# Handing memory and PSUM from the forward to the backward recurrence tile by tile, with the last row sum inside the first backward block and a buffer of its own for the last softmax

## The chip, the cores and the metric

The kernel runs on one core of one Trainium2 chip. The metric is the device time of one execution in microseconds. The core has a matrix engine (TensorE, "PE" in the profile, its weight loads "PEld"), a vector engine (VectorE, "DVE"), an activation engine (ScalarE, "ACT"), a general engine (GpSimd, "POOL"), and SyncE ("SP"), which here issues DMA transfers. Each engine works through its own queue of instructions in the order in which they were written; engines wait for each other by semaphores. Matrix products land in PSUM, which has eight banks of 128 partitions by 2 KB; everything else on the core lies in SBUF.

## The reference

What is computed is a forward pass and the gradients of all of its inputs for a given grad_out. The forward pass, cut to what matters (S = 2048 tokens, Dm = 512, 32 heads of 128, M = 8 memory tokens, segments of 32 tokens, F = 1792):

```python
xn  = layernorm(x)
mem = mem0                                  # 8 rows
for s in range(64):                         # segments of 32 tokens
    h = concat(mem, xn[32*s : 32*s+32])     # 40 rows
    q, k, v = h @ Wq, h @ Wk, h @ Wv        # 32 heads of 128
    p = softmax(where(mask, q @ k.T * scale, -1e9))
    o = (p @ v) @ Wo
    mem = o[:8]                             # goes to the next segment
    outs.append(o[8:])
r   = relu(xn @ w1 + b1)
out = x + concat(outs) + (r * r) @ w2 + b2
# then: vjp of all this for grad_out, for x, mem0, Wq, Wk, Wv, Wo, w1, b1, w2, b2
```

The memory rows make the forward pass a chain through 64 segments, and the backward pass a chain through the same segments in reverse order.

## The kernel before

The kernel has four stages, one after the other: the squared-ReLU layer forward and backward; the forward recurrence; the backward recurrence; and the weight gradients as large matrix products (L2042). The 64 segments are worked in 16 blocks of four (SPB = 4, TC = 16). "L" in names such as `l_attn`, `qLN`, `PLL`, `RFL` means work on a block's memory rows and other edges of its segments, done for a whole block at once; "A" means work on the 32 token rows of a segment.

**Order.** Both recurrences are planned with `_Beat` (L487). Each operation has keys for what it reads and writes, and a due time from a table: `_FWD` or `_BWD`, each with three tables, for the middle blocks, the first block and the last one. A value is a due time in nanoseconds times 4, plus in its last two bits the engine that takes the operation, where more than one can. An operation of block b is due at its table value plus b times the beat (58,393 or 64,984 ns). Operations whose predecessors are done are written out in order of due time, and that order is each engine's queue, SyncE's and GpSimd's transfers among them. `plan.at = (block, slot group)` says which block an operation belongs to. There are two plans, one for each recurrence, and the second is written out behind the first.

**Forward, around its end.** `chain` (L1422) does a segment's attention, `l_proj` and `l_attn` (L1376) the memory rows of a block, `blk_out` the block's normalized rows. PA holds in its two halves the transposed token rows of two blocks, the half being the block number modulo 2, and the transposed grad_out of two blocks in the backward pass (names hA and gT). The token rows of the attention's result go to DRAM (S_RO) in parts; `out_sum(b)` (L1331) loads them back into `sumR` in two halves, adds them on GpSimd (L1338, L1340) to the rows of the other branch (`sumB`, loaded from S_B) and stores the sum as output. For the last block its four transfers are put on GpSimd's queue. `softmax` (L1290) takes the row maximum, subtracts it (L1296), takes the exponential, sums, and divides; in the form for memory rows ("L") the intermediate `st` is not a buffer of its own but `sumR`:

```python
sm_t[sfx] = [... mx, sm ...] + [tl("stA", ...)[:] if sfx == "A" else
                sumR[:].rearrange("p y d -> p (y d)").rearrange("p (i k) -> p i k", i=NI)]
```

so that `out_sum` and the memory rows' softmax share the key `stL`. At the end of the forward plan `turn` (L750) transposes Wv in place, in groups of eight 128x128 matmuls (L688) through a PSUM bank and back by one VectorE or ScalarE copy (L692, L694), and `turn_o` does the same to Wo, with two copies a group. Wo lies in the tile WB, Wq, Wk and Wv in WA.

**Backward.** It begins with 32 such groups for Wk and Wq, of which nine stand ahead of the first matmul of the recurrence and the others among it. `l_pre` (L1671) loads a block's grad_out transposed (`dmaT`, L1666) and does the memory rows' part, `load` (L1789) fetches a segment's q, k, v and softmax, `chain` (L1803) follows a segment backward, `l_post` (L1709) forms a block's gradients for memory rows and stores to S_GN and others; one store to S_RL belongs to each block. The block-diagonal operands BDP, BDL, BDS, BDK are set to zero once (L1619) and then filled by small copies (L928, L934). The weight turns of both plans take PSUM banks from rings.

**Memory.** Each recurrence opens its own SBUF pool (`fw` L1238, `bw` L1587) and its own PSUM pool (`pc`, `pc2` L1589). The second pair takes the space of the first, so the first use of any of its tiles waits for the release of what lay there.

Of the kernel before, what the change touches and what calls it, by code (L numbers as in the profile page):

```python
# [10 lines left out]
ALU = mybir.AluOpType  # L11
# [67 lines left out]
    ),  # L79
    (  # L80
# [82 lines left out]
    ),  # L163
)
_FWD_BEAT = 58393
_BWD = (
    (
# [1937 lines left out]
```

## Time and profile before

| | |
|---|---|
| median of 3 runs | 2857.02 us (2855.41 to 2859.66) |
| the profiled execution's own time | 2858.51 us |
| its span, first to last instruction | 2856.7 us |
| mean granted TensorE clock | 0.994 |
| TensorE busy | 2688.5 us, 94% of the span |
| VectorE, ScalarE, GpSimd busy | 1611.3, 1189.5, 939.8 us |

One execution was recorded by the hardware profiler. Its page gives the busy time of each engine, the span in slices, the chain of work that ended last, and the costliest groups of instructions by source line. Beside the page the trace can be asked for the timeline of an engine in a stretch of time, for what each engine waited for (and which instruction or transfer released it), and for a table of stretches with each engine's busy time, the granted clock as a share of full speed, the DMA share and GB/s. Times count from the start of the span. In a timeline a line is: start, duration, engine, source line, operation, output <- inputs, shape, count, and in brackets the idle time before it with its releaser. "SPq" is a transfer's issue on SyncE's queue.

### The profile page before, as it was taken

How to read it: one execution, taken by the hardware profiler on the slowest of the kernel's cores; microseconds unless marked ns; L12 is line 12 of the kernel's file. 1: busy time of each engine (PE TensorE's matmuls, PEld its weight loads, DVE VectorE, ACT ScalarE, POOL GpSimd, SP SyncE). 2: the span in 40 equal slices, each digit the busy share in tenths (PEclk: the TensorE clock that was granted, in tenths of full speed). 3: DMA queues.
4: the chain of work that ended last, by engine and by line, in shares of the span. 5: the costliest groups of instructions: out<-in, count | busy, mean ns of one | idle time of the engine just before them, and what ended most of it. 6: DMA issues, size and time to landing. Idle time of an engine off the chain costs nothing. (4 is left out here: it accounts for less than half of the span.)

```text
span 2856.7 us, 113933 instructions
## 1 busy us (share of the span) xinstructions
PE 2688.5 (94%) x47469; PEld 1556.2 (54%) x47640; DVE 1611.3 (56%) x4769; ACT 1189.5 (42%) x2781; POOL 939.8 (33%) x2630
## 2 busy tenths in 40 slices
PE   8998999999999999789999999999999899999999
PEld 6664565555656555565555555555555444444444
DVE  5645667666666667566566666666666602232322
ACT  4333455455545555455555555555555400000000
POOL 1102223222322223344455554545454301111111
PEclk9999999999999999999999999999999999999999
DMA  6657768777777765368889898888888799788861
GB/s 195 213 170 200 199 196 215 207 199 200 207 203 210 200 187 165 118 149 216 221 230 240 226 236 235 232 224 232 221 233 214 207 358 298 229 255 266 253 185 43
DMA packets 557595, 606.26 MB, mean 212 GB/s; under 512 B 229925, under 2 KB 358454, under 8 KB 555030
## 3 DMA queue, kind: packets, MB, share of 16 engines
q1 hardware_dynamic: 541654, 544.09, 69.0%
q0 software_dynamic: 15424, 54.87, 5.7%
q8 instruction: 374, 6.13, 1.0%
q14 instruction: 143, 1.17, 0.2%
HBM read 290.14 MB, written 272.12 MB: 197 GB/s over the span
## 5 line engine op out<-in xcount | busy, mean ns | idle before, releaser
L802 PE MATMUL ps<-WA,PA 128*32 128x512 bf16 x6144 | 366.8, 379 | 5.5 <-DVE PA L1490 3.7
L2042 PE MATMUL ps<-WA,WB 128*128 128x512 bf16 x1505 | 330.7, 379 | 2.2 <-DVE gwo L692 0.6
L802 PEld LDWEIGHTS <-PA 128*32 128x32 bf16 x8192 | 207.3, 96 | 202.5 <-issue 12.2
L2042 PEld LDWEIGHTS <-WB 128*128 128x128 bf16 x1896 | 185.5, 98 | 224.4 <-issue 0.9
L692 DVE CAST gwo<-ps 128x512 bf16<-128x512 f32 x64 | 40.0, 683 | 398.9 <-PE ps L2042 267.2
L1660 PE MATMUL ps<-WA,dT 128*32 128x512 bf16 x4096 | 248.2, 382 | 9.7 <-DVE dT L785 8.0
L694 ACT CAST dN<-ps 128x512 bf16<-128x512 f32 x356 | 206.0, 586 | 108.9 <-PE ps L912 77.3
L694 ACT CAST gwo<-ps 128x512 bf16<-128x512 f32 x64 | 33.1, 599 | 517.2 <-PE ps L2042 357.9
L928 POOL COPY BDA<-PB 32x128 bf16<-32x128 bf16 x287 | 82.6, 288 | 413.8 <-DVE PLp L1458 266.8
L2053 POOL DMA_DIRECT2D out_dram<-gwo x96 | 71.3, 751 | 294.2 <-ACT gwo L694 263.4
L1660 PEld LDWEIGHTS <-dT 128*32 128x32 bf16 x4096 | 94.2, 97 | 125.8 <-DVE dT L785 46.8
L785 DVE STREAM_TRANSPOSE dT<-dN 128x256 f32<-128x256 f32 x256 | 109.4, 434 | 68.3 <-ACT dN L694 65.8
L934 POOL COPY BDL<-dSL 32x64 bf16<-32x64 bf16 x256 | 61.5, 240 | 255.9 <-PE ps L912 234.3
L1316 PE MATMUL ps<-WB,OT 128*32 128x256 bf16 x4096 | 134.1, 278 | 5.0 <-DVE OT L785 4.7
L802 PE MATMUL ps<-WB,PA 128*32 128x512 bf16 x2048 | 125.5, 381 | 6.6 <-issue 5.8
L1660 PE MATMUL ps<-WA,gOT 128*32 128x512 bf16 x2048 | 128.0, 380 | 1.2 <-DVE gOT L785 0.9
L934 POOL COPY BDP<-bP 32x256 bf16<-32x256 bf16 x256 | 106.7, 417 | 67.7 <-ACT BDP L928 16.3
L1542 PE MATMUL ps<-sx,anT 128*128 128x512 bf16 x352 | 116.1, 380 | 10.5 <-issue 4.3
L1316 PEld LDWEIGHTS <-OT 128*32 128x32 bf16 x4096 | 101.6, 98 | 42.2 <-DVE OT L785 32.5
L694 ACT CAST gON<-ps 128x512 bf16<-128x512 f32 x123 | 72.0, 585 | 107.7 <-PE ps L802 96.6
L928 POOL COPY BDS<-maskA 32x128 bf16<-32x128 bf16 x249 | 72.0, 289 | 128.4 <-DVE maskA L1846 122.6
L802 PE MATMUL ps<-WA,PB 128*32 128x512 bf16 x1536 | 113.4, 380 | 0.0
(320 smaller groups left out, 5753.8 us busy)
## 6 DMA issues: line engine op xcount, KB each, us to landing
S_GN<-dN SPq DMA_DIRECT2D x192, 256.0 KB
WA<-S_GN SPq DMA_DIRECT2D x160, 256.0 KB
S_K<-kN SPq DMA_DIRECT2D x64, 256.0 KB
S_Q<-qN SPq DMA_DIRECT2D x64, 256.0 KB
S_V<-vN SPq DMA_DIRECT2D x64, 256.0 KB
S_ON<-oN SPq DMA_DIRECT2D x64, 256.0 KB
bqN<-S_Q SPq DMA_DIRECT2D x64, 256.0 KB
xs<-S_Q SPq DMA_DIRECT2D x64, 256.0 KB
```

The costliest lines, as they stand in the source:

```text
L692: nc.vector.tensor_copy(out, in_)
L694: nc.scalar.copy(out, in_)
L785: self.plan.add({"DVE": 0.36}, lambda e, x=x: nc.vector.transpose(dst[:, x, :, :].rearrange("p i c r -> p (i c r)").bitcast(F32).rearrange ...
L802: nc.tensor.matmul(bk()[32 * j:32 * (j + 1), :], lhsT=win(dc), rhs=Wt(dc, c0), start=(dc == 0), stop=(dc == DC - 1), tile_position=(0, 32 ...
L928: self.plan.add({"ACT": 0.31, "DVE": 0.2, "POOL": 0.31}, lambda e, j=j: {"ACT": nc.scalar.copy, "DVE": nc.vector.tensor_copy, "POOL": nc.g ...
L934: self.plan.add(cost or {"ACT": 0.4, "DVE": 0.27, "POOL": 0.42}, lambda e, j=j: {"ACT": nc.scalar.copy, "DVE": nc.vector.tensor_copy, "POO ...
L1316: nc.tensor.matmul(bk()[32 * t:32 * (t + 1), :], lhsT=tq(OTt, i, j), rhs=Wo[:, JQ * i + j, h * HB:(h + 1) * HB], start=(i == 0 and j < 2), ...
L1542: A(pe(0.217, "f", 0.11), lambda e, c=c, z=z, x=x: nc.tensor.matmul(bks[x]()[:], lhsT=anT[x][:, c, :], rhs=sx[z][:], start=(c == 0), stop= ...
L1660: nc.tensor.matmul(bk()[32 * j:32 * (j + 1), :], lhsT=tq(XT, i, j), rhs=wtf(t, i, j), start=(first and i == 0), stop=(last and i == NI - 1 ...
L2042: nc.tensor.matmul(bks[n]()[:], lhsT=HNc[:, rc, dc * P:(dc + 1) * P], rhs=half_of(gns[y], hf), start=(y == 0), stop=(y == NRC - 1))
L2053: q.dma_start(outWs[t][dc * P:(dc + 1) * P, hf, :, j], wt[:].rearrange("p (i e) -> p i e", i=4))
```

## The change

- **Tiles that live through both recurrences.** One SBUF pool `px` and one PSUM pool with all eight banks (`ps_all`) are opened before the forward recurrence and closed after the backward one. The tiles of px have neutral names: XK (2), XA, XN (8), XH (3), BDA, BDB, PLp. Forward names (KT, qLT, vLN, lN, PLL, sumR, sumB, hN, anT, sx, wt) and backward names (gN, qN, kN, VR, VT, Pt, btA, PLL, VTL, kLN, LT, dN, dT, gOT, xs, ys, R_A, BDL, BDK) are views of them; `dSp` is PLp, BDP and BDS are BDA and BDB. The pools `fw` and `bw` keep what is left.
- **Last sum.** `out_sum(15)` is taken out of the last forward block and put at the start of the backward plan, in the first block's table under a slot group of its own (`plan.at = (0, -2)`). Its transfers are on SyncE's queue.
- **Last softmax.** In block 15 the memory rows' softmax takes `stX`, the first part of anT (tile XA), in place of the buffer that `out_sum` uses.
- **Parity.** The backward halves are chosen by (b + 1) % 2 in place of b % 2, so that block 15's transposed grad_out goes to the half of PA that block 14 had.
- **Zeroing.** Of the four memsets of BDP, BDL, BDS, BDK two are left (BDL, BDK), written in the forward plan's last block; those of dSp go. The mask's scratch tile mk becomes a view of WA.
- **Tables.** The tables are given anew in steps a hundred times finer (beats 5,839,300 and 6,498,400). The forward middle table is the old one times 100, for a fifth of its values up to rounding, and orders the operations as before. The tables of the first and last forward block and all backward tables differ in order; in a middle backward block 27 operations change engine.

The diff, cut to its core:

```diff
-    with tc.tile_pool(name="fw", bufs=1) as fw, \
-            tc.tile_pool(name="pc", bufs=1, space=bass.MemoryType.PSUM) as pc:
+    px_cm = tc.tile_pool(name="px", bufs=1)
+    px = px_cm.__enter__()
+    pc_cm = tc.tile_pool(name="pc", bufs=1, space=bass.MemoryType.PSUM)
+    pc = pc_cm.__enter__()
+    ps_all = pc.tile([P, 8, 512], F32, name="ps")
+    XK = [px.tile([P, SPB * NI * JQ * KA], BF16, name="XK%d" % x) for x in range(2)]
+    XA = px.tile([P, 7 * HW], BF16, name="XA")
+    XN = [px.tile([P, HW], BF16, name="XN%d" % x) for x in range(8)]
+    XH = [px.tile([P, HW // 2], BF16, name="XH%d" % x) for x in range(3)]
+    BDA, BDB = (px.tile([P, NI, JQ, RA], BF16, name=n) for n in ("BDA", "BDB"))
...
+    def out_sum(sg, b, sumR, rk, sumB, bk):
+        A = sg.plan.add
+        sumR = sumR[:].bitcast(F32).rearrange("p (y d) -> p y d", y=2)
+        sg.dma(lambda: sumB, lambda: S_B[b * P:(b + 1) * P, :], [], bk)
+        for h in range(2):
+            sg.dma(lambda h=h: sumR, lambda h=h: S_RO[b, h].rearrange("y p d -> p y d"),
+                   [("RO", b, v) for v in range(SPB)] + [("RO", b, "L")], [rk])
+            A({"POOL": 0.9}, lambda e: nc.gpsimd.tensor_tensor(
+                out=sumR[:, 0, :], in0=sumR[:, 0, :], in1=sumR[:, 1, :], op=ALU.add), [], [rk])
+            A({"POOL": 0.9}, lambda e, h=h: nc.gpsimd.tensor_tensor(
+                out=sumB[:, h * HB:(h + 1) * HB], in0=sumR[:, 0, :], in1=sumB[:, h * HB:(h + 1) * HB], op=ALU.add),
+              [rk], bk)
+        sg.dma(lambda: out0flat[b * P:(b + 1) * P, :], lambda: sumB, bk, [])
+
+    with tc.tile_pool(name="fw", bufs=1) as fw:
...
+        stX = XA[:, 0:HW].bitcast(F32).rearrange("p (i k) -> p i k", i=NI)
...
+            if own:
+                st, k = stX, lambda n: ("anT", 0, 0) if n == "st" else n + sfx
...
-            softmax("L", bk, 2 * RL, PLL, "PLL", 1, (0.72, 0.64, 0.71))
+            softmax("L", bk, 2 * RL, PLL, "PLL", 1, (0.72, 0.64, 0.71), b == TC - 1)
...
-            out_sum(b, tail)
+            if not tail:
+                out_sum(sg, b, XN[7], "stL", XH[1][:], ["sumB"])
...
+        BDL, BDK = (tr4(XK[0], x * HW) for x in range(2))
+        for x, t_ in enumerate((BDL, BDK)):
+            A({"POOL": 0.95}, lambda e, t_=t_: nc.gpsimd.memset(t_, 0.0), ...)
...
-    pc2_cm = tc.tile_pool(name="pc2", bufs=1, space=bass.MemoryType.PSUM)
-    pc = pc2_cm.__enter__()
...
-        for t_ in (BDP, BDL, BDS, BDK):
-            nc.gpsimd.memset(t_[:], 0.0)
+        BDP, BDS = BDA, BDB
...
         def l_pre(b):
             plan.at = (TC - 1 - b, 0)
-            p = b % 2
+            p = (b + 1) % 2
...
+        plan.at = (0, -2)
+        out_sum(sg, TC - 1, xs[0], ("xs", 0), XN[6][:, 0:D], [("ys", 0), ("ys", 1)])
         sg.rings = {"t": [("c", 4), ("f", 1)], "f": [("f", 0)]}
         for t, nm in ((1, "Wk"), (0, "Wq")):
             sg.turn("t", nm, Wqkv[t], nm, (t, "WT"))
         l_pre(TC - 1)
```

More of the change, by code (lines that the diff above doesn't have):

```diff
@@ L967 @@
     NEG = -1e9
[L968 to L969 removed]
+    mk = WA[:, 0:RA]
+    nc.gpsimd.memset(mk, 0.0)
     for j in range(JQ):
@@ new lines, with nat, tr4 @@
+    PLp = []
+    for v in range(SPB):
+        t_ = (px.tile([P, NI, RL], BF16, name="PLp%d" % v)[:] if v + 1 < SPB else
+              pb_rest[:, HW // 2:HW // 2 + NI * RL].rearrange("p (i k) -> p i k", i=NI))
+        if v + 1 < SPB:
+            nc.vector.memset(t_, 0.0)
+        PLp.append(t_)
+    def nat(t, at=0):
+        return t[:, at:at + HW].rearrange("p (i e) -> p i e", i=NI)
+    def tr4(t, at=0):
+        return t[:, at:at + HW].rearrange("p (i j r) -> p i j r", i=NI, j=JQ)
+    def out_sum(sg, b, sumR, rk, sumB, bk):
[11 more added lines that the diff above has]
+        sg.dma(lambda: out0flat[b * P:(b + 1) * P, :], lambda: sumB, bk, [])
@@ L1254 @@
         xL = inL
-        KT = [tl("KT%d" % x, [P, SPB, NI * JQ, KA]) for x in range(2)]
-        qLT = [tl("qLT%d" % x, TR) for x in range(2)]
-        vLN = [tl("vLN%d" % x, NAT) for x in range(2)]
-        lN0, lN1 = (tl(n, NAT) for n in ("lN0", "lN1"))
+        KT = [XK[x][:].rearrange("p (v a k) -> p v a k", v=SPB, k=KA) for x in range(2)]
+        qLT = [tr4(XN[x]) for x in range(2)]
+        vLN = [nat(XN[2 + x]) for x in range(2)]
+        lN0, lN1 = nat(XN[4]), nat(XN[5])
         VM = lN1
@@ L1264 @@
         PTA, PTL = (pb_rest[:, x * HW // 4:(x + 1) * HW // 4].rearrange("p (i k) -> p i k", i=NI) for x in range(2))
-        PLL, PTLL = tl("PLL", [P, NI, 2 * RL]), tl("PTLL", [P, NI, 2, RL])
-        BDA, BDB = (tl(n, [P, NI, JQ, RA]) for n in ("BDA", "BDB"))
+        PLL = XN[6][:, 0:HW // 2].rearrange("p (i k) -> p i k", i=NI)
+        PTLL = XN[6][:, HW // 2:HW].rearrange("p (i c k) -> p i c k", i=NI, c=2)
         for t_ in (BDA, BDB):
             nc.gpsimd.memset(t_[:], 0.0)
-        RFA, RFL = tl("RFA", [P, HB], F32), tl("RFL", [P, HB], F32)
+        RFA, RFL = tl("RFA", [P, HB], F32), XH[0][:].bitcast(F32)
         selF = tl("selF", [P, 2 * M], F32)
@@ L1277 @@
             )
-        sumR, sumB = tl("sumR", [P, 2, HB], F32), tl("sumB", [P, D])
-        hN = tl("hN", [P, D])
+        hN = XH[2]
         sm_t = {}
@@ L1282, with softmax @@
             sm_t[sfx] = [tl(n + sfx, [P, NI], F32) for n in ("mx", "sm")] + [tl("stA", [P, NI, nk], F32)[:] if sfx == "A" else
-                            sumR[:].rearrange("p y d -> p (y d)").rearrange("p (i k) -> p i k", i=NI)]
+                            XN[7][:].bitcast(F32).rearrange("p (i k) -> p i k", i=NI)]
+        stX = XA[:, 0:HW].bitcast(F32).rearrange("p (i k) -> p i k", i=NI)
         plan = _Beat(tc, _FWD_BEAT, TC, _FWD)
-        sg = Stage(plan, {"c": (0, 4), "f": (4, 2), "m": (6, 2)}, pc.tile([P, 8, 512], F32, name="ps"), 0.9)
+        sg = Stage(plan, {"c": (0, 4), "f": (4, 2), "m": (6, 2)}, ps_all, 0.9)
         A = plan.add
         V = nc.vector
-        def softmax(sfx, bk, nk, Pout, pkey, prio, cA):
+        def softmax(sfx, bk, nk, Pout, pkey, prio, cA, own=False):
             mx, sm, st = sm_t[sfx]
@@ L1329, in wo_part @@
                   [bk.key], [(okey, half)], prio, 0.07)
-        def out_sum(b, tail):
-            q = "POOL" if tail else "SP"
-            c = T_DMA + tail
-            sg.dma(lambda: sumB[:], lambda: S_B[b * P:(b + 1) * P, :], [], ["sumB"], cost=c, eng=q)
-            for h in range(2):
-                sg.dma(lambda h=h: sumR[:], lambda h=h: S_RO[b, h].rearrange("y p d -> p y d"),
-                       [("RO", b, v) for v in range(SPB)] + [("RO", b, "L")], ["stL"], cost=c, eng=q)
-                A({"POOL": 0.9}, lambda e: nc.gpsimd.tensor_tensor(
-                    out=sumR[:, 0, :], in0=sumR[:, 0, :], in1=sumR[:, 1, :], op=ALU.add), [], ["stL"])
-                A({"POOL": 0.9}, lambda e, h=h: nc.gpsimd.tensor_tensor(
-                    out=sumB[:, h * HB:(h + 1) * HB], in0=sumR[:, 0, :], in1=sumB[:, h * HB:(h + 1) * HB], op=ALU.add),
-                  ["stL"], ["sumB"])
-            sg.dma(lambda: out0flat[b * P:(b + 1) * P, :], lambda: sumB[:], ["sumB"], [], cost=c, eng=q)
         def l_proj(b):
@@ L1417, in l_attn @@
             sg.dma(lambda: S_RO[b].rearrange("h y (v r) d -> (h y) v r d", r=RA)[:, :, 0:M],
-                   lambda: RFL[:], ["RFL"] + [("RO", b, v) for v in range(SPB)], [("RO", b, "L")],
+                   lambda: RFL, ["RFL"] + [("RO", b, v) for v in range(SPB)], [("RO", b, "L")],
                    cost=T_DMA + tail, eng="POOL" if tail else "SP")
-            out_sum(b, tail)
+            if not tail:
+                out_sum(sg, b, XN[7], "stL", XH[1][:], ["sumB"])
         def chain(s):
@@ L1520, in blk_out @@
                        cost=T_DMA + tail, eng="POOL" if tail else "SP")
-        anT = [tl("anT%d" % x, [P, TC, P]) for x in range(2)]
-        sx = [tl("sx%d" % x, [P, D]) for x in range(5)]
-        wt = tl("wt", [P, D])
-        wtT = wt[:].rearrange("p (c f) -> p c f", c=DC)
+        anT = [XA[:, 2 * HW * x:2 * HW * (x + 1)].rearrange("p (c f) -> p c f", c=TC) for x in range(2)]
+        sx = [XA[:, 4 * HW + x * D:4 * HW + (x + 1) * D] for x in range(5)]
+        wt = XA[:, 4 * HW + 5 * D:7 * HW]
+        wtT = wt.rearrange("p (c f) -> p c f", c=DC)
         def dw_unit(which, u):
@@ L1582 @@
         plan.at = (TC - 1, -1)
+        BDL, BDK = (tr4(XK[0], x * HW) for x in range(2))
+        for x, t_ in enumerate((BDL, BDK)):
+            A({"POOL": 0.95}, lambda e, t_=t_: nc.gpsimd.memset(t_, 0.0), [("KTL", 0, 0)] if x else [],
+              [("KTL", 0, h) for h in range(2)] + [("KTA", 0, v, h) for v in range(SPB) for h in range(2)] if x == 0 else [("bd", 1)])
         sg.turn("m", "Wv", Wqkv[2], ("WA", 2), "WvT")
@@ L1596 @@
         TR = [P, NI, JQ, RA]
-        dSp = []
-        for v in range(SPB):
-            t_ = (tl("dSp%d" % v, [P, NI, RL])[:] if v + 1 < SPB else
-                  pb_rest[:, HW // 2:HW // 2 + NI * RL].rearrange("p (i k) -> p i k", i=NI))
-            nc.vector.memset(t_, 0.0)
-            dSp.append(t_)
+        dSp = PLp
         gT = inA
         gL = inL
-        qLN, kLN, gLN = ([tl(n + "%d" % x, NAT) for x in range(2)] for n in ("bqLN", "bkLN", "gLN"))
-        VTL = [tl("VTL%d" % x, TR) for x in range(2)]
@@ L1607 @@
-        PLL, dSL = ([tl(n + "%d" % x, [P, NI, 2 * RL]) for x in range(2)] for n in ("bPLL", "dSL"))
-        LT0, LT1, LT2 = (tl("LT%d" % x, TR) for x in range(3))
-        VTM, VR = LT1, tl("VR", TR)
+        at = lambda x, n: XA[:, x:x + n]
+        halves = lambda t: t.rearrange("p (i k) -> p i k", i=NI)
+        gN, qN, kN = (nat(XA, x * HW) for x in range(3))
+        VR = tr4(XA, 3 * HW)
+        VT = at(4 * HW, NI * JQ * KA).rearrange("p (i j k) -> p i j k", i=NI, j=JQ)
+        x0 = 4 * HW + NI * JQ * KA
@@ new lines @@
+        Pt = [halves(at(x0 + x * NI * KA, NI * KA)) for x in range(2)]
+        btA = halves(at(x0 + 2 * NI * KA, 2 * NI * KA).bitcast(F32))
+        x0 += 4 * NI * KA
+        PLL = [halves(at(x0, HW // 2)), halves(XH[1][:])]
+        assert x0 + HW // 2 == 7 * HW
+        dSL = [tl("dSL", [P, NI, 2 * RL])[:], halves(XH[0][:])]
+        qLN, gLN = ([tl(n + "%d" % x, NAT)[:] for x in range(2)] for n in ("bqLN", "gLN"))
+        VTL, kLN = [tr4(XK[0], 2 * HW), tl("VTL", TR)[:]], [nat(XK[0], 4 * HW), tl("bkLN", NAT)[:]]
@@ L1610 @@
+        LT0, LT1, LT2 = tr4(XK[1]), tr4(XK[0], 3 * HW), tr4(XN[3])
+        VTM = LT1
         dLN = tl("dLN", NAT)
         KM = dLN
-        dSTLL = tl("dSTLL", [P, NI, 2, RL])
+        dSTLL = XH[2][:].rearrange("p (i c k) -> p i c k", i=NI, c=2)
         brL = tl("brL", [P, NI], F32)
-        xs = [tl("xs%d" % x, [P, HW]) for x in range(JQ)]
+        xs = [XN[x] for x in (1, 4, 5, 7)]
         btL = xs[3][:].bitcast(F32).rearrange("p (i k) -> p i k", i=NI)
-        ys = [tl("ys%d" % x, [P, NI * RL]) for x in range(JQ)]
@@ L1617 @@
-        BDP, BDL, BDS, BDK = (tl(n, [P, NI, JQ, RA]) for n in ("BDP", "BDL", "BDS", "BDK"))
-        for t_ in (BDP, BDL, BDS, BDK):
-            nc.gpsimd.memset(t_[:], 0.0)
-        qN, kN, gN = (tl(n, NAT) for n in ("bqN", "bkN", "gON"))
-        VT, gOT = tl("bVT", [P, NI, JQ, KA]), tl("gOT", TR)
-        Pt = [tl("bP%d" % x, [P, NI, KA]) for x in range(2)]
-        btA, brA = tl("btA", [P, NI, KA], F32), tl("brA", [P, NI], F32)
+        ys = [XN[6][:, x * NI * RL:(x + 1) * NI * RL] for x in range(JQ)]
```

50 lines of the change are left out of this document (22 added, 28 removed), and 601 rows, old and new, of tables (_BWD, _FWD).

## The prediction

> **What bounds the kernel now.** I read the page first for the engine that sets the time, then the table of stretches for the place where that engine stops, then the timelines of TensorE, VectorE and SyncE at that place.
>
> ```profile
> span 2856.7 us, 113933 instructions
> PE 2688.5 (94%) x47469; PEld 1556.2 (54%) x47640; DVE 1611.3 (56%) x4769; ACT 1189.5 (42%) x2781; POOL 939.8 (33%) x2630
> ```
>
> TensorE is busy for 94% of the span, so a change can win only where TensorE stands still. The table of stretches (busy time of TensorE, its weight loads, VectorE, ScalarE, GpSimd, then the granted clock) shows where that is:
>
> ```profile
> 1130.00:1190.00 60.00, 51.88 (x1260) 33.85 (x1249) 39.48 (x118) 28.52 (x66) 19.67 (x55) 1.00 0.38 122
> 1340.00:2250.00 910.00, 856.06 (x19484) 497.43 (x19484) 579.43 (x1811) 495.99 (x1150) 458.89 (x1420) 1.00 0.87 229
> 1193.60:1201.90 8.30, 0.06 (x1) 0.00 (x0) 1.30 (x3) 0.58 (x2) 2.14 (x4) 0.67 0.53 159
> 1211.50:1228.40 16.90, 9.56 (x132) 8.71 (x129) 11.27 (x19) 7.99 (x15) 5.36 (x8) 0.86 0.21 59
> 1228.40:1236.20 7.80, 7.01 (x72) 6.43 (x71) 3.72 (x7) 2.02 (x2) 4.66 (x5) 0.65 0.90 134
> 1236.20:1265.40 29.20, 27.91 (x606) 20.59 (x606) 22.72 (x54) 18.11 (x28) 11.84 (x38) 1.00 0.74 182
> ```
>
> The steady backward recurrence (second row) runs at 94%. The seam between the recurrences does not: TensorE works 0.06 us of 8.30 just before 1201.9, then 9.56 us of 16.90 in the turn of Wo. The change edits that seam. Its TensorE timeline (start, duration, line, operation, in brackets the idle time ahead and what ended it):
>
> ```profile
> 1193.05 0.61 PE L688 MATMUL ps<-ident,WA 128*128 128x128 bf16 x8 [0.31 <-ACT WA L694]
> 1201.94 1.01 PE L688 MATMUL ps<-ident,WA 128*128 128x128 bf16 x8 [8.28 <-DVE WA L692]
> 1207.67 0.24 PE L868 MATMUL ps<-vLN,PTLL 32*32 32x128 bf16 x4
> 1211.53 2.41 PE L688 MATMUL ps<-ident,WB 128*128 128x128 bf16 x40
> 1217.58 4.09 PE L688 MATMUL ps<-ident,WB 128*128 128x128 bf16 x48 [2.40 <-ACT WB L694]
> 1228.43 2.80 PE L688 MATMUL ps<-ident,WA 128*128 128x128 bf16 x24 [1.59 <-DVE WB L692]
> 1236.23 0.62 PE L802 MATMUL ps<-WB,PB 128*32 128x512 bf16 x8
> ```
>
> So the path here is: eight idle microseconds, rest of the forward pass (1201.94 to 1211.53), Wo's turn (1211.53 to 1228.43), nine Wk groups (1228.43 to 1236.23), first backward chain. What holds TensorE at 1193.7 is a queue behind a queue, read from the other engines' timelines and the table of waits (total, times, longest):
>
> ```profile
> 1191.33 0.69 DVE L1295 TENSOR_REDUCE mxL<-ps 128x8 f32<-128x512 f32 x1
> 1200.60 0.69 DVE L1296 TENSOR_TENSOR sumR<-ps,mxL 128x512 f32<-128x512 f32 x1 [8.58 <-POOL sumB L1340]
> 1199.10 0.72 POOL L1338 TENSOR_TENSOR sumR<-sumR 128x256 f32<-128x256 f32 x1 [3.87 <-DMA sumR<-S_RO]
> 1199.90 0.67 POOL L1340 TENSOR_TENSOR sumB<-sumR,sumB 128x256 bf16<-128x256 f32 x1
> 1196.16 0.41 SPq L748 DMA_DIRECT2D sumR<-S_RO  x1
> 1192.09 1.50 SPq L1667 DMA_TRANSPOSE PA<-in_grad_out_dram  x1
> SPq L1667 <- PE ps L688: 16.2, 1, 16.2
> SPq L748 <- DMA out_dram<-sumB: 18.4, 1, 18.4
> 1228.64 0.32 SPq L748 DMA_DIRECT2D bqN<-S_Q  x1
> 1228.40 0.94 POOL L1619 MEMSET BDP<- 128x1024 bf16 x1 [1.62 <-DVE WB L692]
> ```
>
> SyncE stands 16.2 us at the transposing load of block 15's gradient, because that load's half of PA is still read by block 15 itself. Behind it in SyncE's queue lies the second load of out_sum(14) (1196.16). GpSimd adds it into sumR until 1200.5, and sumR is also the buffer in which the last softmax subtracts its maximum (L1296). VectorE waits in order, the Wv evictions behind it wait, TensorE finds no free bank. The second SyncE row is the other barrier: the first backward load (1228.64) stood 18.4 us for the pools that the forward recurrence gives up, until out_sum(15) had stored its rows.
>
> **The change, part by part.** Own softmax buffer and turned block parity. The last softmax writes anT's first part, unused by then, and block 15's gradient goes to the half of PA that block 14 has left. Both locks go together: L1296 can follow L1295 at 1192.0 instead of 1200.6, 8.6 us earlier; the parity removes what would be late next, the VM loads and out_sum(14)'s load behind SyncE's block. After 1201.94 nothing was waiting for anything but this (forward matmuls and the softmax chain), so the stretch from 1201.94 to 1211.53 moves as a whole: lower end 8.3 us (the idle time), upper end 8.6 plus what the slow clock cost. For that, two rows of the same matmul shape and the clock:
>
> ```profile
> 1188.46 0.62 PE L1316 MATMUL ps<-WB,OT 128*32 128x256 bf16 x16
> 1202.88 1.04 PE L1316 MATMUL ps<-WB,OT 128*32 128x256 bf16 x16
> 1200.00:1210.00 10.00, 7.14 (x156) 5.21 (x159) 6.59 (x12) 4.58 (x7) 3.03 (x6) 0.67 0.55 187
> ```
>
> At 0.62/1.04 the 7.14 us of TensorE work in that row would be 4.3: up to 2.9 us more. I take 9.0 in all, since the softmax chain on VectorE and ScalarE, not TensorE's rate, orders most of those 10 us. Ends: 8.3 and 11.5.
> [...]
>
> Shared tiles and banks, so no barrier between pools. Before, the nine Wk groups belong to the second plan and follow Wo's turn. In the written order of the changed program 6 of the 9 lie between Wo's groups and only 3 behind them, then the first chain. Wo's turn itself had room: 16.90 us with 9.56 of TensorE, 11.27 of VectorE, 7.99 of ScalarE. The 6 groups bring 6 evictions and two thirds of 7.01 us of matmul at clock 0.65, about 3.0 us at full clock. VectorE and ScalarE did 3.72 + 2.02 = 5.74 us in the row of the nine groups, so six cost at most 3.8 on the two. Free time there is 5.6 us of VectorE, 8.9 of ScalarE, 7.3 of TensorE, so they fit: cost 0, or 1.9 if both evicting engines are the bound in turn. Behind the turn, 3 groups take a third of 7.80, 2.6 us: 5.2 gained. Net 5.2 at the best, 3.3 at the worst; I take 4.5, nearer the best because the free time is twice the need.
> The loads that began at 1228.64 and the memsets from 1228.40 are hidden then: two memsets are left of four GpSimd ones (0.94 each) and lie in idle GpSimd time. The four VectorE memsets of dSp go too. That earlier loads help the first block (1236.20 to 1265.40, TensorE 27.91 of 29.20) I count as 0: at most 1.3 us of idle time could go. If a load comes late in the new order instead, it costs up to one landing, 2.9 us (SyncE's 1196.16 to GpSimd's 1199.10).
>
> out_sum(15). Its two store-gated loads, the load of S_B and the store move from GpSimd's queue (at the tail) to SyncE's, its four adds into the first backward block. GpSimd: 2 x (0.72 + 0.67) = 2.8 us in a stretch where it is busy 11.84 of 29.20; hidden, upper end 2.8. SyncE: four issues of about 0.4, and the first S_RO load stands behind RFL's store on GpSimd, with kN, P and qN loads queued behind it. Before, that store stood here:
>
> ```profile
> 1212.68 0.55 POOL L748 DMA_DIRECT2D S_RO<-RFL  x1 [1.33 <-DMA S_ONL<-lN]
> ```
>
> It was issued 1.2 us after Wo's turn began (1211.53); with the landing of 2.9 SyncE's queue holds until some 4 us into the turn, 15 us before the first chain asks (16.9 + 2.6 - 4). Cost taken: 0.5, ends 0 and 2.8.
> [...]
>
> Planned order. The general forward table is the old one times 100, so forward middle blocks stay. The backward tables are new: in a middle block about 10 of 483 TensorE steps change place, a net four small operations per block come to VectorE from GpSimd (3) and ScalarE (1), and SyncE's stores of S_GON, S_R, S_GOA and S_DSL move among the loads.
>
> ```profile
> L1971 SPq DMA_DIRECT2D ga<-S_RL x64: 264/294/3530, 2354.6 to 2762.6; - x64
> L748 SPq DMA_DIRECT2D S_RL<-xs x15: 319/394/415, 1361.5 to 2271.3; - x15
> PE ps L1760 <- DMA ys<-S_PL: 5.5, 6, 1.5
> PE ps L1660 <- DVE dT L785: 5.4, 17, 1.3
> PE ps L912 <- POOL BDL L934: 3.7, 12, 0.4
> ```
>
> The beat is (2271.3 - 1361.5)/14 = 64.99 us. In the 800 us from 1400 to 2200 these three greatest waits sum to 14.6 us, 1.2 per block; removing them all would win 17 us in 14 blocks, and doubling them would lose as much. With 2% of TensorE's order changed I take 0, and 0.25 us per block either way, that is 3.5, for the range. End of the backward pass and first forward block: 0, 2 either way.
>
> Sum against the profiled execution: 9.0 + 4.5 - 0.5 = 13.0 us of gain. The profiled execution took 2858.51, so 2845.5; it stands 1.5 us above the median of the runs, 2857.02, on which the same gain gives 2844.0.
>
> **The rivals.** First, the gain stays at the wait. The 8.3 us go, but Wo's turn, with six groups more, becomes longer by what the nine groups lose, because its banks alternate between VectorE and ScalarE in fixed order (the 2.40 us idle "<-ACT WB" is such a wait). Then 2857.0 - 8.3 + 0.5 = 2849.2. For it: idle time in the turn is made of evictions in series. Against: both engines are idle a third of the time.
> Second, the other side: the new backward order loses. If a GpSimd or ScalarE copy now ends last in each segment, each of the 14 x 4 segments is late by some tenths; the gain of 13.0 is gone at 13.0/56 = 0.23 us per segment, the length of one such copy (the BDL row's longest single wait is 0.4). At 0.4 us per segment the time would be 2844.0 + 22.4 = 2866.4. For it: about 27 operations per block change engine, and 94% busy leaves 3.9 us of slack per block. Against: 98% of TensorE's order stays.
> Third, more than I sum: the clock term in full (11.5), the groups in full (5.2), the first block's idle 1.3, nothing for out_sum, and a backward order better by 0.25 us per block: 2857.0 - 18.0 - 3.5 = 2835.5.
> Fourth, the change doesn't do what it says: some other lock, such as the S_VM stores that the VM loads wait for, ends at 1200 as well, and the seam keeps its length: 2857.
>
> **How the numbers follow.** My forecast 0.50, first rival 0.16, second 0.13, third 0.15, fourth 0.06. The predicted time is 2844.0. Its own range, from the ends of its terms and the 3.5 of the order, is 2837 to 2852. The range for 8 in 10 is 2834 to 2855: it holds the third and the first rival and leaves out most of the second and the fourth. A measurement of this kernel tells about 0.2%, 5.7 us, from no change, so faster means below 2851.3: the forecast, the third and most of the first rival, 0.77. Same: a part of the first, the fourth, and a mild form of the second, 0.12. Slower 0.11.
>
> **What the profile after would show.** Right: no idle time of 8 us on TensorE between Wv's groups; L1296 straight behind L1295; SyncE without the stands of 16.2 and 18.4; the first L802 of the backward pass about 13 us earlier; S_RL stores 65.0 us apart. A step is wrong if Wo's turn takes over 20 us, if the first chain waits for a load queued behind S_RO, or if GpSimd's adds are named as releaser of a TensorE wait in the first block. The whole is wrong if the distance of the S_RL stores grows by 0.9 us (4 segments at 0.23), whatever the seam has won.

## The result, and the profile after

Over 20 runs each, the changed kernel takes 2863.12 us (2854.62 to 2876.0) and the kernel before 2854.95 us (2841.39 to 2865.47): ratio 1.0036, 95% interval 1.0023 to 1.0048. The change makes the kernel slower by about a third of a per cent; 2844.0 was forecast. The profiled execution of the changed kernel took 2858.24 us, near the fast end of its runs, and that of the kernel before 2858.51, so the two traces look alike in total. They are not alike inside.

The page of the changed kernel first, then its timelines of TensorE, VectorE and GpSimd at the seam (line numbers of its own file: L757 is L688 of before, L871 is L802, L1396 and L1397 are L1295 and L1296, L1487 is L1400):

```profile
span 2856.5 us, 114006 instructions
PE 2690.7 (94%) x47470; PEld 1553.5 (54%) x47640; DVE 1632.8 (57%) x4814; ACT 1168.5 (41%) x2761; POOL 929.7 (33%) x2595
```

```profile
1188.71 0.30 PE L1487 MATMUL ps<-XK,XN 128*32 128x64 bf16 x16
1198.21 2.66 PE L757 MATMUL ps<-ident,WB 128*128 128x128 bf16 x40
1215.79 0.61 PE L871 MATMUL ps<-WB,PB 128*32 128x512 bf16 x8
1189.07 0.69 DVE L1396 TENSOR_REDUCE mxL<-ps 128x8 f32<-128x512 f32 x1
1189.80 0.69 DVE L1397 TENSOR_TENSOR XA<-ps,mxL 128x512 f32<-128x512 f32 x1
1235.90 0.73 POOL L1338 TENSOR_TENSOR XN<-XN 128x256 f32<-128x256 f32 x1
1236.71 0.67 POOL L1340 TENSOR_TENSOR XN<-XN,XN 128x256 bf16<-128x256 f32 x1
```

At the seam everything forecast is there. The subtraction follows the maximum at once, Wo's turn begins at 1198.21 and the first backward matmul at 1215.79 (1236.23 before). The loss is behind it. The S_RL stores of the changed kernel, first and last by the view of that tile and two single ones by SyncE's timeline; then the same two single stores of the kernel before:

```profile
L817 SPq DMA_DIRECT2D S_RL<-XN x15: 376/383/936, 1345.7 to 2267.9; - x15
L817 POOL DMA_DIRECT2D S_RL<-XN x1: 566/566/566, 2302.6 to 2302.6; - x1
1411.49 0.38 SPq L817 DMA_DIRECT2D S_RL<-XN  x1
2202.31 0.38 SPq L817 DMA_DIRECT2D S_RL<-XN  x1
```

```profile
1429.05 0.39 SPq L748 DMA_DIRECT2D S_RL<-xs  x1
2198.75 0.40 SPq L748 DMA_DIRECT2D S_RL<-xs  x1
1190.96 0.30 PE L1400 MATMUL ps<-KT,qLT 128*32 128x64 bf16 x16
L748 POOL DMA_DIRECT2D S_RL<-xs x1: 557/557/557, 2302.6 to 2302.6; - x1
```

The second to the fourteenth S_RL store span twelve blocks that only the middle table orders. Call a twelfth of it the middle distance: (2198.75 - 1429.05)/12 = 64.14 us before, (2202.31 - 1411.49)/12 = 65.90 us after. In stages, from the last scores of block 15's memory rows (L1400, L1487):

| stretch, us | before | after |
|---|---|---|
| to the start of Wo's turn | 20.6 | 9.5 |
| Wo's turn to the first backward L802 | 24.7 | 17.6 |
| to the first S_RL store | 125.3 | 129.9 |
| first to last S_RL store | 941.1 | 956.9 |

The seam and the first block win 170.6 - 157.0 = 13.6 us. The backward blocks lose 15.8, and 17.6 in a second trace of the changed kernel (2311.0 - 1352.3 = 958.7):

```profile
L817 SPq DMA_DIRECT2D S_RL<-XN x15: 319/382/1639, 1352.3 to 2277.9; - x15
L817 POOL DMA_DIRECT2D S_RL<-XN x1: 563/563/563, 2311.0 to 2311.0; - x1
```

The 15.8 are 21.1 lost in the twelve middle blocks, 8.7 won in the first and the last of the store distances (140.1 to 131.4), and 3.4 lost in the last one of all (31.3 to 34.7). The rest of the difference lies ahead of the last scores. The first trace of the changed kernel reaches them 2.2 us sooner than the kernel before, so that its total is even. The second reaches them 2.3 us later, wins 11.5 at the seam and the first block, and is 8.1 us longer in all, like the medians. Versions with the same forward part reach their last scores anywhere from 1188.7 to 1199.7, so no cause is claimed for that part.

One trace is one sample: traces of two versions told below, with the old tables on the old tiles, have a middle distance of 64.83 and 64.76, so 64.14 is at the low end, and the second trace of the changed kernel has 66.29. By these the loss per middle block is 1.1 to 2.2 us, not 1.76 to the hundredth.

### The profile page after: what moved, and what is told of

Read it like the earlier page. It is cut to its first block, busy times and chain, and to the rows that moved or that the text cites. A ratio compares the mean times of both kernels' runs of the same rounds, so it can differ in the third digit from the quotient of the medians.

```text
span 2856.5 us, 114006 instructions
## 1 busy us (share of the span) xinstructions
PE 2690.7 (94%) x47470; PEld 1553.5 (54%) x47640; DVE 1632.8 (57%) x4814; ACT 1168.5 (41%) x2761; POOL 929.7 (33%) x2595
## 4 chain that ended last, share of the span: by engine, by line
PE 28%; issue 10%; DVE 8%; DMA 5%; POOL 2%; ACT 2%; SPq 0%; DVEq 0%; POOLq 0%; ACTq 0%
PE ps L2137 12%; PE ps L1752 7%; PE ps L871 3%; PE ps L981 3%; DMA S_GN<-XK 1%; DMA WA<-S_GN 1%; DVE maskA L1938 1%; PE ps L757 1%; DVE XN L854 1%; DMA XN<-S_PL 1%; PE ps L1967 1%; DVE XA L1936 1%; DVE XN L761 1%; DVE PB L1943 1%; DVE PB L1942 1%
## 5 line engine op out<-in xcount | busy, mean ns | idle before, releaser
L871 PE MATMUL ps<-WA,PA 128*32 128x512 bf16 x6144 | 367.2, 380 | 4.7 <-DVE PA L1578 3.8
L1752 PE MATMUL ps<-WA,XK 128*32 128x512 bf16 x5120 | 319.3, 383 | 5.5 <-DVE XK L854 3.4
L871 PEld LDWEIGHTS <-PA 128*32 128x32 bf16 x8192 | 206.9, 96 | 202.3 <-issue 15.7
L763 ACT CAST XK<-ps 128x512 bf16<-128x512 f32 x313 | 180.4, 587 | 102.5 <-PE ps L981 42.1
L1752 PEld LDWEIGHTS <-XK 128*32 128x32 bf16 x5120 | 117.9, 97 | 145.6 <-DVE XK L854 44.8
L1752 PE MATMUL ps<-WA,XN 128*32 128x512 bf16 x2560 | 168.2, 382 | 0.5 <-issue 0.2
L761 DVE COPY XN<-ps 128x256 f32<-128x256 f32 (+1 forms) x148 | 66.5, 450 | 169.7 <-PE ps L757 118.5
L763 ACT CAST XA<-ps 128x512 bf16<-128x512 f32 (+1 forms) x154 | 90.3, 587 | 127.9 <-PE ps L871 114.9
L763 ACT COPY XN<-ps 128x512 bf16<-128x512 bf16 (+1 forms) x156 | 72.6, 477 | 158.1 <-PE ps L1752 54.4
L871 PE MATMUL ps<-WB,PA 128*32 128x512 bf16 x2048 | 127.5, 386 | 9.8 <-issue 9.0
L981 PEld LDWEIGHTS <-XK 128*128 128x128 bf16 x1536 | 95.1, 98 | 69.1 <-issue 21.2
L1630 PE MATMUL ps<-XA 128*128 128x512 bf16 x353 | 115.5, 381 | 10.3 <-issue 4.6
L854 DVE STREAM_TRANSPOSE XK<-XK 128x256 f32<-128x256 f32 x256 | 108.5, 434 | 24.8 <-ACT XK L763 21.9
L1003 POOL COPY BDA<-XA 32x256 bf16<-32x256 bf16 x256 | 107.2, 419 | 46.2 <-POOL XK L1003 13.9
```

Source lines behind the costliest of these rows:

```text
L761: nc.vector.tensor_copy(out, in_)
L763: nc.scalar.copy(out, in_)
L854: self.plan.add({"DVE": 0.36}, lambda e, x=x: nc.vector.transpose(dst[:, x, :, :].rearrange("p i c r -> p (i c r)").bitcast(F32).rearrange ...
L871: nc.tensor.matmul(bk()[32 * j:32 * (j + 1), :], lhsT=win(dc), rhs=Wt(dc, c0), start=(dc == 0), stop=(dc == DC - 1), tile_position=(0, 32 ...
L981: nc.tensor.matmul(bv()[:, n * P:(n + 1) * P], lhsT=B_[:, i, :, :].rearrange("p j k -> p (j k)"), rhs=X[:, i, :], start=(y == 0 and n == 0 ...
L1003: self.plan.add(cost or {"ACT": 0.4, "DVE": 0.27, "POOL": 0.42}, lambda e, j=j: {"ACT": nc.scalar.copy, "DVE": nc.vector.tensor_copy, "POO ...
```

## The experiments

**Each half of the change alone.** The kernel before with the softmax buffer and the parity:

```diff
-            softmax("L", bk, 2 * RL, PLL, "PLL", 1, (0.72, 0.64, 0.71))
+            softmax("L", ..., b == TC - 1)      # st is the first part of anT there
...
-            p = b % 2                           # l_pre, l_post, chain, blk_out
+            p = (b + 1) % 2
```

> The kernel before with two parts of the change alone: the last softmax in a buffer of its own (the first part of anT) and the turned parity of the backward blocks. Pools, order tables and out_sum stay. If the prediction's step is right, the first TensorE idle time of 8.3 us goes and Wo's turn starts 8.3 to 11.5 us earlier: 2857 becomes about 2848 on the same scale, ratio 0.997. Rival: the rest of the forward tail, out_sum(15) on GpSimd and the pool barrier take it back, since the first backward load waits for the output's store: the first L802 of the backward pass moves by less than 3 us, ratio 0.999 to 1.000.

Measured: 2850.55 against 2857.72 us, ratio 0.9975 (0.9962 to 0.9989). From its timeline of TensorE, the last scores, Wo's turn and the first L802:

```profile
1189.82 0.30 PE L1403 MATMUL ps<-KT,qLT 128*32 128x64 bf16 x16
1202.72 2.41 PE L688 MATMUL ps<-ident,WB 128*128 128x128 bf16 x40
1226.55 0.61 PE L802 MATMUL ps<-WB,PB 128*32 128x512 bf16 x8
```

The first stretch is 12.9 us in place of 20.6, a gain of 7.7; the second, 23.8, hardly moves. The 8.3 us of idle time are gone, and up to the first L802 the pool barrier takes nothing back.

The softmax buffer without the parity:

> The kernel before with the softmax buffer of its own alone (parity unchanged). The subtraction L1296 no longer waits for out_sum(14), but SyncE still stands at the gradient's transposing load until block 15 has left that half of PA, with the memory rows' loads behind it. If that is what would be late next, as predicted: TensorE's idle time of 8.3 us shrinks but the matmuls L868 wait for these loads, and Wo's turn starts 3 to 6 us earlier instead of 9 to 11. Rival: the parity adds nothing, and Wo's turn starts as early as with both.

Measured: 2856.13 against 2860.01, ratio 0.9988 (0.9972 to 1.0003). The first stretch is 19.5 us, a gain of only 1.1, less than expected. The subtraction runs at once, but VectorE then stands 5.0 us for the store of hN that lies behind SyncE's stand, and TensorE for the memory rows' loads:

```profile
1191.08 0.69 DVE L1299 TENSOR_TENSOR anT<-ps,mxL 128x512 f32<-128x512 f32 x1
1197.57 0.42 DVE L692 COPY hN<-ps 128x512 bf16<-128x512 bf16 x1 [5.02 <-DMA S_HNA<-hN]
1203.31 0.26 PE L868 MATMUL ps<-lN,PTLL 32*32 32x128 bf16 x1 [1.81 <-DMA lN<-vN]
```

So the root is SyncE's stand at the gradient's load; the shared buffer is only its first victim. The parity alone was not tried.

**The backward order.** The old table of the middle blocks can be put into the changed kernel, since both plans hold the same operations in the same order but for the eight of out_sum(15). First the middle and last tables:

```diff
-_BWD = (new middle, new first, new last)
+_BWD = (old middle, new first, old last)   # old values in the finer steps, plus 4.95 us
```

> The changed kernel with the backward tables of the kernel before for the middle and the last blocks (in the finer steps, shifted as a whole by 4.95 us so that they join the new table of the first block, which stays). Theory A, the new backward order is what costs: the S_RL stores stand 65.0 us apart again, not 65.9, the seam's gain of 15.8 us stays, the last 3 us at the end come back too: about 2840, 14 to 18 below the kernel before. Theory B, the shared tiles are what costs (waits for a neighbour in the same tile): the distance stays near 65.9 and the time near that of the changed kernel. Theory C, an even mix: 65.4, some 7 us below before.

Measured: 2858.17 against 2857.72, ratio 0.9999 (0.9982 to 1.0016): no case of the three. The middle distance falls to 64.65, as theory A had it, but the first S_RL store stands 138.6 us behind the first backward matmul (129.9 in the changed kernel): it seems that the old second block does not join the new first one. With all three old tables:

```diff
+_BWD = (old middle, old first, old last)   # out_sum(15) at its new due times
```

> The changed kernel with all three backward tables of the kernel before (in the finer steps, shifted by 4.95 us), and the eight operations of out_sum(15) at their new due times. If the loss is the new backward order, and joining old middle blocks to the new first block is what spoilt the first mixture, this keeps the shared tiles, the parity, the softmax buffer and the moved sum, and loses nothing behind the seam: last forward block as in the changed kernel (S_ONL 38 to 40 us after the one before it), middle distance of the S_RL stores 64.1 to 64.8, about 2843, ratio 0.994 to 0.996. If the shared tiles cost by themselves: middle distance 65.5 or more, ratio 1.000 or above.

Measured: 2847.21 us (2836.42 to 2862.42) against 2859.55, ratio 0.9955 (0.9939 to 0.9972). This kernel beats both: 12.3 us below the one before on the same chip. Its rows:

```profile
1196.01 0.30 PE L1471 MATMUL ps<-XK,XN 128*32 128x64 bf16 x16
1205.52 2.66 PE L741 MATMUL ps<-ident,WB 128*128 128x128 bf16 x40
1223.89 0.87 PE L855 MATMUL ps<-WB,PB 128*32 128x512 bf16 x8
L801 SPq DMA_DIRECT2D S_RL<-XN x15: 319/389/1397, 1350.1 to 2266.3; - x15
L801 POOL DMA_DIRECT2D S_RL<-XN x1: 566/566/566, 2296.5 to 2296.5; - x1
```

The stretches are 9.5, 18.4, 126.2 and 946.4: nearly all of the seam's gain stays, and the backward blocks lose 5 us, not 16. The middle distance is 65.03, a little above what was expected, and 0.2 above the two versions on the old tiles. The shared tiles and banks therefore cost little; the new backward tables, in which alone this kernel differs from the changed one, cost the rest.

The converse, the kernel before with the new table for the middle blocks alone:

```diff
-_BWD = (old middle, old first, old last)
+_BWD = (new middle, old first, old last)
```

> The kernel before with nothing changed but the table of the middle backward blocks, which is that of the changed kernel. Theory A (order): S_RL stores 65.9 us apart, 12 to 18 us slower than before (about 1.0045). Theory B (shared tiles): 65.0 us apart and no slower than 0.1%.

Measured: 2909.42 against 2857.72, ratio 1.0192 (1.0175 to 1.0209), far more than expected. The middle distance is 66.79, and the joins to the old first and last blocks cost as well: 144.6 us to the first S_RL store and 83.7 for the last distance. It has one gain that was not expected. SyncE issues the gradient's load at 1216.65 here, behind the forward plan's last transfers, where the kernel before has it among them (1192.09). out_sum(14)'s load is not held up, and Wo's turn starts 10.2 us after the last scores although softmax and out_sum share their buffer. That bears out that SyncE's stand is the root.

**Which part of the order.** Four mixtures, in the middle table only. Due times of SyncE's 109 operations old, the rest new; the opposite; old due times with the new choice of engines; the opposite. The first and the fourth keep the new tables of the first and last block, the other two the old ones.

> The changed kernel with the due times of SyncE's 109 operations alone taken from the kernel before in the table of the middle backward blocks; the due times and engines of all others stay new. Theory A1, the transfers' places cost (the loads of S_PL stand too late for L1852, which waits 16 us for them in 800): the distance of the S_RL stores falls to about 65.1 and the waits of L1852 to some 6. Theory A2, the engines of the copies or the order on TensorE cost: it stays above 65.7.

> As the kernel with all old backward tables, but SyncE's 109 operations of the middle blocks have their new due times; everything else is old. If the places of the transfers cost: middle distance of the S_RL stores 65.5 to 66.5, and TensorE waits for the loads of S_PL grow from some 6 us to some 16 in 800. If not: 64.1 to 64.8 and waits of 5 to 8 us.

> As the kernel with all old backward tables, but in the table of the middle blocks the engine of each operation is the new one (27 of about 545 a block) and the due times are the old ones. If the moved copies cost (a slower engine, or an engine's queue in which others wait behind them): middle distance of the S_RL stores 65.5 to 66.5, as with the new table. If the new due times cost: 64.1 to 64.8, as with the old one.

> The changed kernel, new due times everywhere, but in the table of the middle backward blocks the engine of each operation is that of the kernel before. If the moved copies cost: middle distance of the S_RL stores falls from 65.9 to about 64.5. If the due times (order within each queue) cost: it stays at 65.5 or more.

Measured, with the greatest TensorE waits from 1420 to 2200:

| middle table | ratio (95%) | middle distance | greatest waits, us |
|---|---|---|---|
| SyncE old, rest new | 1.0041 (1.0026 to 1.0056) | 66.7 | L1736 for dT's transpose 21.5 |
| SyncE new, rest old | 1.0354 (1.0331 to 1.0377) | 73.6 | L1836 for S_PL 39.8 |
| engines new, due times old | 1.0070 (1.0050 to 1.0091) | 67.1 | L1896 for gOT's copy 21.4 |
| engines old, due times new | 1.0066 (1.0045 to 1.0087) | 67.2 | L1836 for S_PL 20.5 |

Three of the four are worse than either table whole. The first, 1.0041, cannot be told from the changed kernel (1.0036, and 1.0021 in a second set of runs). So these runs do not divide the loss among SyncE's places, due times and engines: a piece of one table put into the other adds losses of its own. A mixture with TensorE's order alone exchanged was not tried.

**The greatest wait of the changed kernel.** Its table of waits of TensorE from 1420 to 2200, then that of the version with old tables (L1852 and L1836 are the matmuls L1760 of `l_post`; in the table above L1736 is L1660 of before, and L1896 is L1820):

```profile
PE ps L1852 <- DMA XN<-S_PL: 9.8, 8, 2.7
PE ps L871 <- issue: 9.0, 6, 2.0
PE ps L1852 <- DMA XH<-S_PLL: 5.5, 3, 2.3
```

```profile
PE ps L1836 <- DMA XN<-S_PL: 8.1, 6, 3.0
PE ps L1736 <- DVE XK L838: 5.8, 13, 1.9
PE ps L965 <- POOL XK L987: 3.0, 11, 0.3
```

The old order waits often and briefly (97 waits, 36 us, in the kernel before), the new one more seldom and longer (67 waits, 47 us). Idle times of TensorE of 1.2 us or more in these 780 us: 6 with 9.0 us before, 14 with 27.4 after, 7 with 12.9 in the version with old tables. The granted clock is below 1.00 behind five of the 14, 1.73 to 3.11 us long (0.66 to 0.78 in the lowest row of 5 us), and behind none of the 6. In the table of stretches by 5 us, around one such gap of the changed kernel:

```profile
1558.93 0.38 PE L871 MATMUL ps<-WB,PA 128*32 128x512 bf16 x1 [1.97 <-issue]
1555.00:1560.00 5.00, 3.03 (x55) 1.53 (x47) 0.95 (x3) 1.83 (x4) 0.00 (x0) 1.00 1.05 342
1560.00:1565.00 5.00, 5.00 (x118) 3.83 (x116) 2.87 (x11) 3.52 (x9) 2.79 (x8) 0.66 0.80 247
```

A clock of 0.66 over 5 us is counted as 5 x (1 - 0.66) = 1.7 us lost, an estimate. Summed so over such rows the clock loses 8.6 us in 780 after and nothing before (every row is at 1.00); with the old tables its mean over the 780 us is 1.00, against 0.99 after. Waits and clock together are 20 us more after than before, in 12 blocks an estimate of 1.7 a block, against 1.76 measured.

A late load is the greatest single wait, so it was issued earlier, in the new order and in the old one:

```diff
-    ... 38789560 ...      # new middle table, last load of S_PL: 96.97 us, 92.0 less the 4.95
+    ... due at 77.0 us    # old middle table: 85.8 to 76.0 us
```

> The changed kernel with one number of its table for the middle backward blocks changed: the last of the loads of S_PL that the memory rows' matmuls L1852 need is due 15 us earlier (77.0 instead of 92.0 us), so that it is issued ahead of a load of q, two stores of S_GN and a load of k instead of behind them. Theory L (this late load is the cause: TensorE waits 16 us for it in 800, and the longest of these waits pull the clock down): waits of L1852 for transfers fall below 5 us, the granted clock from 1420 to 2200 rises from 0.9875 to 0.995 or more, the middle distance of the S_RL stores falls from 65.9 to 64.6 to 65.0, the time by 10 to 16 us against the changed kernel, ratio to before 0.997 to 0.999. Theory O (the order as a whole, no single place): the wait moves to the next late load or copy, the distance stays above 65.5.

> The changed kernel with the old backward tables, and the same single load due 9.8 us earlier (76.0 instead of 85.8) in the middle blocks. There the load is late by less (8 us of waits in 780). Theory L: these waits fall to below 4 us and the time by 2 to 6 us more, ratio to before 0.993 to 0.995. Theory O: no change from 0.9955, within its interval.

> The changed kernel once more, for a second trace on the same chip as the two others of this set. Middle distance of the S_RL stores 65.7 to 66.5, last forward block 38 us, ratio to before 1.002 to 1.005, clock from 1420 to 2200 below 0.993.

Measured in the new order: 2869.55 against 2860.01, ratio 1.0040 (1.0028 to 1.0052), middle distance 66.2. The waits for that load are gone, as both theories had it, and nothing is won:

```profile
PE ps L1896 <- DVE XN L745: 13.2, 9, 3.0
PE ps L965 <- issue: 6.1, 2, 3.2
```

L1896 is the next step of the recurrence; it now waits for gOT's copy on VectorE. In the old order the waits for the load fall from 8.1 to 1.5 us and the ratio is 0.9965 (0.9946 to 0.9984), no better than 0.9955. The changed kernel on the same chip: 2865.37, ratio 1.0021 (1.0006 to 1.0036), middle distance 66.3. Theory L falls.

In this run VectorE's waits name the next in line: a copy of dN, ahead of gOT's copy in its queue, stands for the store S_GN of the dN before it, in the same buffer:

```profile
DVE XK L745 <- DMA S_GN<-XK: 19.4, 10, 3.6
```

With the old tables this is 3.7 us. Of the 24 copies of dN in a block, the old table has one on VectorE and the new one four. The three were put back on ScalarE, with and without the early load, and were put on VectorE in the old order:

```diff
-    engine code 2 (VectorE)   # three slots of the new middle table
+    engine code 1 (ScalarE)   # in the old one the other way round
```

> The changed kernel with the early load of S_PL of the experiment before and, in the table of the middle backward blocks, three evictions of dN per block (part_bd's second half) back on ScalarE, where the kernel before had them; the changed kernel has them on VectorE. Theory Q (two late places of one stretch hide each other: the load of S_PL, and VectorE standing in such an eviction for the store S_GN of the dN before, with gOT's eviction queued behind): with both mended, VectorE's waits for S_GN fall from 19 us in 780 to below 5, TensorE's waits for gOT from 13 to below 4, the granted clock rises above 0.994, the middle distance of the S_RL stores falls to 64.6 to 65.2 and the ratio to before is 0.995 to 0.998. Theory O (the order as a whole): VectorE's waits for S_GN go, but another wait comes up, and the distance stays above 65.6.

> The changed kernel with these three evictions back on ScalarE and the load of S_PL where the change has it. Theory Q: VectorE's waits for S_GN go, but TensorE still waits 16 to 23 us in 780 for the late load, so the distance stays at 65.5 to 66.5 and the ratio at 1.000 to 1.005. Rival: the evictions alone are the cause, and the distance falls to 65.2 or less.

> The fast version (old backward tables on the shared tiles), with only these three evictions per block put on VectorE. Theory Q: VectorE's waits for S_GN grow from 3.7 us in 780 to more than 10, the middle distance grows by 0.5 us or more from 65.0 and the ratio from 0.9955 to 0.998 or above. Theory O: no change beyond 0.2 us of distance.

Measured: with both, 2864.25 against 2856.47, ratio 1.0031 (1.0014 to 1.0049), middle distance 65.95. VectorE's waits for S_GN are gone, ScalarE has them instead, and TensorE waits one step later, for the transpose of that dN:

```profile
ACT XK L747 <- DMA S_GN<-XK: 36.3, 20, 4.0
PE ps L1736 <- DVE XN L838: 16.8, 10, 3.2
```

Without the early load: ratio 1.0047 (1.0026 to 1.0068), distance 66.5, 14.5 us of waits for S_PL. In the old order VectorE's waits for S_GN grow to 9.7 us, and the ratio, 0.9974 (0.9957 to 0.9992), and the distance, 64.8, cannot be told from that version's own (0.9955 and 65.03). Theory Q falls too.

What stands: at one place of each block the load of S_PL, the copy and the transpose of dN (held by the store S_GN) come late together in the new order, and taking away one, or two, lets TensorE run into the next. That the new backward tables as a whole cost the time is shown; which of their due times or engines would have to change is open.

## Why the prediction was wrong

**Own softmax buffer and turned parity** (9.0, ends 8.3 and 11.5): right in mechanism. Wo's turn begins 11.1 us earlier; 7.7 of it come from these two parts alone, a little under the lower end, the rest with the other parts in place. That the parity removes what would be late next was right and is the greater half: the buffer alone gives 1.1. Wo's turn, all of it transposes, ran at a granted clock of 1.00 (0.86 before):

```profile
1200.00:1210.00 10.00, 9.22 (x139) 8.02 (x136) 9.27 (x16) 6.68 (x11) 3.35 (x8) 1.00 0.79 193
```

The kernel before has transposes at both clocks: in its nine Wk groups (1228.43 to 1236.23, transposes alone) the clock is 0.50 to 0.56 in the rows of 1 us up to 1234 and 1.00 in the two behind them.

**Shared tiles and banks, Wk's groups in Wo's turn** (4.5, ends 3.3 and 5.2): right in kind, undersized; the stretch shrank by 7.1, and by 6.3 in the second trace. The turn with its six groups took 15.7 us, where 16.9 was taken over unchanged, and the three groups 1.9 instead of 2.6, at a granted clock of 1.00 where the two stretches before had 0.86 and 0.65.

**First block and out_sum(15)** (0 and 0.5): the first block took 4.6 us more. GpSimd's four adds last 0.67 to 0.73 us as before, and no TensorE wait names them. The prediction also allowed for a load that comes late in the new order, at up to one landing of 2.9, and counted it as nothing. One does come late here, 3.6 us, and 2.6 in the second trace; no trace with all old tables has this wait in its first block:

```profile
1313.52 0.46 PE L1852 MATMUL ps<-XN,XN 128*32 128x128 bf16 x10 [3.55 <-DMA XA<-S_PLL]
```

But the kernel before with only the buffer and the parity shows 129.7 us without it, and three versions with the same old table for this block 125.3, 126.2 and 129.0, so most of the 4.6 is within what traces differ by. Its cause is not settled, and the price of out_sum was not measured by itself. These steps together were forecast at 13.0 and measured at 13.6 (11.5 in the second trace). That they agree is in part luck: the two gains were 18.2 where 13.5 was forecast, and the first block took 4.6 where 0.5 was.

**Planned order** (0, ends 3.5 either way): this is the step that failed. It was priced by TensorE's order, of which 2% changed, with the words "With 2% of TensorE's order changed I take 0". The tables also moved the copies, transposes and transfers to other queues and places. Seven of TensorE's fourteen long waits name a load or a copy; for the other seven the trace shows no releaser ("issue"), and what holds them is open. The prediction had a better figure in hand: it worked out that doubling its three waits would lose 17 us in 14 blocks, and then set the bound at 3.5 with no reason but the 2%. (Its three waits were not quite the greatest: TensorE's 3.8 us at L802, put down to "issue", stood third, and all waits together were 36 us in 780, not 14.6.) The step measured 15.8 us of loss in one trace and 17.6 in the other, four and a half to five times its bound.

**The rivals.** The second, the other side, is what happened in kind. In the middle blocks 1.76 us per block is 0.44 per segment, near the 0.4 for which it was worked out. By the prediction's own measure, the fourteen distances from the first to the fifteenth store, 64.99 grows to (2267.9 - 1345.7)/14 = 65.87, by 0.88, just at its sign of 0.9, since the two outer distances became shorter. Its mechanism was another: not a copy that ends last in each segment, but about one long wait in each block (14 of 1.2 us or more in 780 us), and the clock behind some of them. It was given a chance of 0.13, and its reason against, that 98% of TensorE's order stays, did not carry the price.

## What to carry to other kernels

Where a stage of many repeats gets a newly planned order, price that order by its repeats first: a gain of 13.6 us at a seam that runs once was lost to some 1.8 us in each of twelve blocks. Look at what changes in the queues of the engines and transfers around the bounding engine, not only in its own. Removing the greatest wait of a tightly packed block can gain nothing when the next queue is late by as much (the 9.8 us of waits for S_PL went, and the ratio stayed at 1.0040): the experiment that showed the cause put the whole old order back.

## What the runs showed of the hardware

The granted clock fell after idle times far shorter than the 8.28 us of the seam (there 0.50 in rows of 1 us from 1197 to 1206): 0.66 over 5 us behind a gap of 1.97 us, and likewise behind four others of 1.73 to 3.11 us (0.70 to 0.78 in the lowest row of 5 us), though not behind every one (1.00 behind 2.66 us at 1711.89). In rows of 1 us the dip behind the 1.97 us is at 0.50 from 1561 to 1563 and back at 1.00 from 1564, while the gap had ended at 1558.93. In the steady backward blocks, with transfers at 0.87 of the engines' time, the load of S_PL for which TensorE waited was issued 4.6 to 6.3 us before the matmuls could start (eight waits of the changed kernel), against 2.9 us from issue to use for the load of S_RO at the quieter seam (a share of 0.53).
